# Thirty small loads added to a bandwidth-bound decode layer: fifteen ahead of the last head's K, fifteen behind the down weights

## The chip, the cores and the metric

The kernel runs on one core of one Trainium2 chip. The metric is the device time of one execution in microseconds (us); lower is better. A core has five engines, each with its own instruction stream: TensorE (PE in the profile, its weight loads as PEld), VectorE (DVE), ScalarE (ACT), GpSimd (POOL) and SyncE (SP). In this kernel SP computes nothing: it issues every transfer between the device memory (HBM) and the on-chip memory (SBUF, 128 partitions, here called rows of a tile). The transfers are carried by 16 DMA engines, which the profile reports together.

## The reference

One token is decoded through an attention block and a gated feed-forward block, with a residual around each. All is float32.

```
def _A_ref(x, k_cache, v_cache, wq, wo):
    B, Sq, D = x.shape
    H, Dh = 32, 192
    q = (x @ wq).reshape(B, Sq, H, Dh) -> (B, H, Sq, Dh)
    scores = einsum("bhqd,bhkd->bhqk", q, k_cache) * (Dh ** -0.5)
    p = softmax(scores, axis=-1)
    o = einsum("bhqk,bhkd->bhqd", p, v_cache)
    return o -> (B, Sq, H * Dh) @ wo

def _B_ref(x, W_gate, W_up, W_down):
    gate = einsum("bsd,df->bsf", x, W_gate)
    up = einsum("bsd,df->bsf", x, W_up)
    gate = gate * (gate > 0)
    return einsum("bsf,fd->bsd", gate * up, W_down)

h = x + _A_ref(layernorm(x), ...)
h2 = h + _B_ref(layernorm(h), ...)
```

(The transposes are written here as arrows.) The sizes are D = 640, 32 heads of 192, 8192 cached positions for each head, and a feed-forward width of 1536. The K and V caches are 6.3 MB a head each, over 400 MB together. Every byte of them is used once.

## The kernel before, in words

**Tiling.** The host packs all inputs into a few arrays of 128 rows (`row_p`, `row_1` to `row_5`, `row_t1`, `row_t2a`, `row_t2b`, `row_t3`, `row_up`, `row_gate`, `row_down`), so that one DMA takes one long contiguous piece from each row into each of the 128 partitions. In SBUF there are three slots of 65,280 bytes a partition, X, Y and Z (`slot_x`, `slot_y`, `slot_z`). K, V and the weights of a head live in pieces of these slots, and a piece is overwritten as soon as the engines have read it.

**The loop.** Head 0 is done ahead. A loop of ten turns does heads 1 to 30, three a turn, with five loads a turn of 7.6 to 8.2 MB each. Then comes a tail that is written out: the last head's K and the first part of the V of the head before it (`row_t1`, into X), more V and an output weight (`row_t2a`, into Z), the first half of the last head's V (`row_t2b`, into Z behind it), the second half (`row_t3`, into Y), the feed-forward's up weights (`row_up`, Y), its gate weights (`row_gate`, X), and its down weights in four pieces (`row_down`, X).

**Who waits for whom.** Each load has a semaphore that rises to 16 when its data have landed, and each reader waits for it (`land`, `tl`). In the other direction an engine that has read a piece raises a semaphore (`free`, `fin`), and SP waits for it ahead of the load that overwrites the piece. SP's program is a list in this order, and one waiting instruction holds all loads behind it. `sync_program` is that list, `load` issues one DMA, and `turn(i)` issues a turn's loads 3, 4 and 5 and then waits for the two semaphores (`free[2]`, `free[4]`) that release X and Z to the loads that follow.

**TensorE.** `pe_k` computes a half of a head's scores (12 matmuls), `pe_v` the product of the probabilities with V, 32 blocks of 384 columns a head, any stretch of them from `i0` to `i1`; it can raise a semaphore with one of its matmuls (`inc_at`). In the tail `pe_v(vz, 0, 16)` reads the first half of the last head's V from Z, and it is the last reader of Z. The output is 640 numbers in `o2`, copied by DVE and ACT (semaphore `fout`), and stored by SP in a transfer of two rows.

Of the kernel before, what the change touches and what calls it, by code (L numbers as in the profile page):

```python
# [88 lines left out]
def build(nc, arrays):  # L89
    dram = {k: nc.dram_tensor(k, v.shape, F32, kind="ExternalInput").ap() for k, v in arrays.items()}  # L90
    out = nc.dram_tensor("out", (1, 1, D), F32, kind="ExternalOutput").ap()
    sb = lambda name, shape: nc.alloc_sbuf_tensor(name, list(shape), F32).ap()

    slot_w = 16320
    X, Y, Z = (sb(n, [P, slot_w]) for n in ("slot_x", "slot_y", "slot_z"))
# [23 lines left out]
    gu = sb("gu", [P, FG])  # L119
    guT = sb("guT", [P, FJ, 32])  # L120
    o2 = sb("o2", [P, 2 * DG])

    ps = lambda name, w: nc.alloc_psum_tensor(name, [P, w], F32).ap()
    sc = ps("sc", 1024)
# [2 lines left out]
    sem = nc.alloc_semaphore  # L127
# [3 lines left out]
    free = [sem(f"free{i}") for i in range(6)]  # L131
    tl = {n: sem(f"tl_{n}") for n in ("t1", "t2a", "t2b", "t3", "up", "gate", "d0", "d1", "d2", "d3")}
    fin, fout, hsem = (sem(n) for n in ("fin", "fout", "hsem"))
    cst_pe, cst_ve, hdve, hrs, out_s = (sem(n) for n in ("cst_pe", "cst_ve", "hdve", "hrs", "out_s"))

    def wait(eng, s, n, sub=0, **kw):
        w = eng.wait_ge(s, n)  # L137
        if sub:
            w.then_inc(s, -sub)
        return w  # L140

    def op(ins, w=None, inc=None):
        if w is not None:
            ins._wait_ge(*w)
        if inc is not None:
            ins.then_inc(inc, 1)
        return ins
# [22 lines left out]
    vz = lambda i: cut(Z, W_T2A + i * PW, PW) if i < 16 else cut(Y, (i - 16) * PW, PW)  # L170
# [16 lines left out]
    def pe_v(blk, i0, i1, last=None, inc_at=None):  # L187
        for i in range(i0, i1):
            g = i % 4
            m = te.matmul(po[32 * g:32 * g + 2, 0:PW], p[:, 2 * i:2 * i + 2], blk(i), start=(i < 4), stop=(i >= 28))  # L190
            if inc_at is not None and i == inc_at[0]:
                op(m, inc=inc_at[1])
            if i == 31 and last is not None:
                op(m, inc=last)
# [60 lines left out]
    def tensor_program():  # L255
# [21 lines left out]
        wait(te, a2p, 1, 1)  # L277
        pe_l()
        wait(te, tl["t2b"], 16, 16)
        pe_v(vz, 0, 16)  # L280
        wait(te, d2p, 3, 3)
        for g in range(4):
            te.matmul(acc[Q(g), 0:DG], ones[Q(g), 0:32], xd[Q(g)].rearrange("p c j -> p (c j)"),
# [289 lines left out]
    sp = nc.sync  # L573

    def load(t, src, s):
        sp.dma_start(t, src).then_inc(s, 16)

    def sync_program():
        r1, r2, r3, r4, r5 = (dram[f"row_{i}"] for i in range(1, 6))

        def turn(i):
            wait(sp, free[5], 1, 1)
            wait(sp, land[5], 16, 16)
            load(Y[:, 0:W_3], r3[i], land[3])
            wait(sp, free[1], 2, 2)
            load(X[:, 0:W_4], r4[i], land[4])
            wait(sp, free[3], 2, 2)
            load(Y[:, 0:W_5], r5[i], land[5])
            wait(sp, free[2], 1, 1)
            wait(sp, free[4], 1, 1)  # L590

        with sp.Fori(0, NTURN - 1) as i:
            turn(i)
            load(X[:, 0:W_1], r1[i + 1], land[1])
            load(Z[:, 0:W_2], r2[i + 1], land[2])
        turn(NTURN - 1)
        load(X[:, 0:W_T1], dram["row_t1"], tl["t1"])
        load(Z[:, 0:W_T2A], dram["row_t2a"], tl["t2a"])
        load(Z[:, W_T2A:W_T2A + W_T2B], dram["row_t2b"], tl["t2b"])
        wait(sp, free[5], 1, 1)  # L600
        wait(sp, land[5], 16, 16)
        load(Y[:, 0:W_T3], dram["row_t3"], tl["t3"])
        load(Y[:, W_T3:W_T3 + W_UP], dram["row_up"], tl["up"])
        wait(sp, fin, 1, 1)
        load(X[:, 0:W_UP], dram["row_gate"], tl["gate"])
        for n, (a, b) in enumerate(DOWN):
            load(X[:, W_UP + a:W_UP + b], dram["row_down"][:, a:b], tl[f"d{n}"])
        wait(sp, fout, 2)
        load(out[0, 0].rearrange("(g n) -> g n", g=2), o2[31:33, :], out_s)
        wait(sp, fout, 2, 2)  # L610
        wait(sp, out_s, 16, 16)

    programs = ((ET.PE, tensor_program), (ET.DVE, vector_program), (ET.Activation, scalar_program),
                (ET.Pool, pool_program), (ET.SP, sync_program))
    load(Y[:, 0:W_P], dram["row_p"], land[5])
    load(X[:, 0:W_1], dram["row_1"][0], land[1])
# [16 lines left out]
```

## Time and profile before

| what | value |
|---|---|
| median of 3 runs | 1037.67 us (1037.61 to 1037.70) |
| the profiled execution's own time | 1037.78 us |
| its span, first to last instruction | 1036.5 us |
| read from HBM | 445.94 MB, 430 GB/s over the span |
| SP's DMA queue, share of 16 engines' span | 99.6% |
| PE busy | 548.8 us (53%) |
| DVE busy, ACT busy | 188.4 us (18%), 41.5 us (4%) |

How to read it: the span is what the trace covers, and the profiled execution took 1.28 us more than its span, spent ahead of the first and behind the last traced instruction. "SPq" is a row of SP's own instruction stream, "DMA_DIRECT2D" a DMA being issued, and its duration is the time in which SP issues it, not the time of the transfer. "To landing" counts from that issue until the last of the transfer's semaphore counts has come. A window's "DMA share" is the time of the packets that start in it, over 16 engines; a packet here is one row's piece, or the four bytes of a semaphore count. A short window in which many long packets start can show a share above 1.

### The profile page before, as it was taken

The numbers are of one execution on the slowest core, as the hardware profiler recorded it, in microseconds if no ns is written. First come the engines' busy times: TensorE is split into PE (matmuls) and PEld (weight loads), VectorE is DVE, ScalarE is ACT, GpSimd is POOL, SyncE is SP. The second block draws the span as 40 slices with busy tenths as digits, with TensorE's granted clock in tenths as the row PEclk, the third lists the DMA queues.
The fourth block names the chain that finished last, engine by engine and source line by source line (L and its number), as shares of the span: only waits on it lengthen the run. The fifth ranks groups of instructions, "written<-read, shape, count | busy, mean of one in ns | idle before, by whom it ended". The sixth has DMA issues, their size and how long they took to land. (4 is left out here: it accounts for less than half of the span.)

```text
span 1036.5 us, 10312 instructions
## 1 busy us (share of the span) xinstructions
PE 548.8 (53%) x4532; PEld 182.0 (18%) x4532; DVE 188.4 (18%) x479; ACT 41.5 (4%) x138; POOL 2.0 (0%) x13
## 2 busy tenths in 40 slices
PE   0745546455474463564644636646455465464667
PEld 0211112111121121121111202211111111121123
DVE  1301211111222022121111220211222012111211
ACT  1000000000000000000000000000000000000000
POOL 0000000000000000000000000000000000000000
PEclk9877867868776687687676876767767767678698
DMA  9999999999999999999999999999999999999998
GB/s 403 441 433 428 432 436 432 441 423 436 429 444 423 439 438 432 423 443 434 436 423 442 431 438 432 426 435 441 427 428 436 439 425 432 441 432 440 422 426 352
DMA packets 8796, 446.07 MB, mean 430 GB/s; under 512 B 978, under 2 KB 1108, under 8 KB 1236
## 3 DMA queue, kind: packets, MB, share of 16 engines
q1 hardware_dynamic: 8788, 445.95, 99.6%
q8 instruction: 7, 0.11, 0.0%
q14 instruction: 1, 0.01, 0.0%
HBM read 445.94 MB, written 0.00 MB: 430 GB/s over the span
## 5 line engine op out<-in xcount | busy, mean ns | idle before, releaser
L183 PE MATMUL sc<-slot_x,qs 128*32 128x512 f32 x1008 | 147.1, 727 | 88.1 <-PEq L137 88.1
L190 PE MATMUL po<-slot_y,p 128*2 128x384 f32 x1152 | 126.2, 594 | 83.7 <-DMA slot_y<-row 79.3
L190 PE MATMUL po<-slot_z,p 128*2 128x384 f32 x560 | 68.3, 638 | 103.9 <-PEq L137 103.9
L183 PE MATMUL sc<-slot_y,qs 128*32 128x512 f32 x288 | 56.2, 944 | 85.4 <-PEq L137 85.4
L190 PE MATMUL po<-slot_x,p 128*2 128x384 f32 x336 | 43.6, 652 | 82.0 <-PEq L137 82.0
L406 DVE STREAM_TRANSPOSE st<-sc 128x512 f32<-128x512 f32 x64 | 45.7, 713 | 168.7 <-PE sc L183 168.7
L183 PEld LDWEIGHTS sc<-slot_x,qs 128*32 128x32 f32 x1008 | 36.0, 131 | 169.1 <-issue 168.7
L190 PEld LDWEIGHTS po<-slot_y,p 128*2 128x2 f32 x1152 | 32.9, 98 | 177.2 <-DMA slot_y<-row 88.4
L394 DVE COPY oc<-od 128x2 f32<-128x2 f32 x32 | 5.1, 159 | 225.6 <-PE od L209 225.6
L412 DVE TENSOR_REDUCE m<-pt 128x1 f32<-128x128 f32 x32 | 9.3, 292 | 193.6 <-PE pt L202 193.6
L190 PEld LDWEIGHTS po<-slot_z,p 128*2 128x2 f32 x560 | 14.8, 99 | 148.0 <-issue 146.7
L518 ACT COPY qs<-q_ps 128x96 f32<-128x96 f32 x32 | 7.6, 238 | 772.6 <-PE q_ps L199 772.6
L388 DVE SCALAR_TENSOR_TENSOR prod<-slot_y,xn,prod 128x192 f32<-128x192 f32 x88 | 36.9, 419 | 3.1
L183 PEld LDWEIGHTS sc<-slot_y,qs 128*32 128x32 f32 x288 | 13.0, 157 | 114.7 <-issue 114.7
L401 DVE RECIPROCAL rl<-pl 128x1 f32<-128x1 f32 x32 | 5.4, 168 | 130.7 <-PE pl L214 128.0
L183 PE MATMUL sc<-slot_z,qs 128*32 128x512 f32 x240 | 27.6, 592 | 0.0
L190 PEld LDWEIGHTS po<-slot_x,p 128*2 128x2 f32 x336 | 9.0, 95 | 105.1 <-issue 105.1
L206 PE MATMUL od<-mrl,ob 128*128 128x1 f32 x132 | 20.0, 256 | 8.7 <-PEq L137 8.7
L206 PEld LDWEIGHTS od<-mrl,ob 128*128 128x128 f32 x132 | 17.6, 194 | 34.0 <-issue 34.0
L521 ACT COPY ob<-po 128x384 f32<-128x384 f32 x32 | 15.3, 478 | 177.0 <-PE po L190 177.0
L386 DVE TENSOR_SCALAR prod<-slot_y,xn 128x192 f32<-128x192 f32 x22 | 6.9, 315 | 67.2 <-DMA slot_y<-row 67.2
L197 PE MATMUL q_ps<-pat,prod 128*128 128x96 f32 x64 | 15.3, 322 | 7.1 <-PEq L137 7.1
(101 smaller groups left out, 262.6 us busy)
## 6 DMA issues: line engine op xcount, KB each, us to landing
slot_x<-row SPq DMA_DIRECT2D x10, 8160.0 KB, 26.8
slot_z<-row SPq DMA_DIRECT2D x10, 8160.0 KB, 45.7
slot_y<-row SPq DMA_DIRECT2D x10, 8160.0 KB, 45.3
slot_x<-row SPq DMA_DIRECT2D x10, 7680.0 KB, 35.6
slot_y<-row SPq DMA_DIRECT2D x10, 7584.0 KB, 26.9
slot_x<-row_t SPq DMA_DIRECT2D x1, 7680.0 KB, 26.3
slot_y<-row_p SPq DMA_DIRECT2D x1, 7136.0 KB, 19.8
slot_z<-row_t2a SPq DMA_DIRECT2D x1, 5088.0 KB, 38.3
```

Source lines behind the costliest of these rows:

```text
L183: m = te.matmul(sc[Q(g), half * 512:half * 512 + 512], qs[:, 32 * part:32 * part + 32], blk(half, part * 4 + g), start=(part == 0), stop=( ...
L190: m = te.matmul(po[32 * g:32 * g + 2, 0:PW], p[:, 2 * i:2 * i + 2], blk(i), start=(i < 4), stop=(i >= 28))
L197: te.matmul(q_ps[:, 0:96], prod[:, 0:P], pat[:, 0, :], start=True, stop=False)
L206: te.matmul(od[:, 0:1], ob[:, k * DH:k * DH + P], mrl[:, k:k + 1], start=(k == 0), stop=(k == 1))
L386: dv(ve.tensor_scalar(prod, w3[:, 0, :], xn[:, 0:1], None, op0=ALU.mult), w=first)
L388: dv(STT(prod, w3[:, j, :], xn[:, j:j + 1], prod, op0=ALU.mult, op1=ALU.add), w="self", inc=d2p if j == DJ - 1 else None)
L394: dv(ve.tensor_copy(oc, od[:, 0:2]), w=pd())
L401: dv(ve.reciprocal(vec["rl"], pl[:, 0:1]), w=pd())
L406: return dv(ve.transpose(st[:, s], sc[:, s]), w=w)
L412: dv(ve.reduce_max(vec["m1"], pt[:, 0:P], axis=AX.X, negate=True), w=pd(), inc=d2a)
L518: op(ac.copy(qs, q_ps[:, 0:96]), w=ap("p2a"), inc=a2p)
L521: op(ac.copy(ob, po[:, 0:PW]), w=ap("p2a"), inc=a2p)
```

## The change

Two groups of 15 DMAs are put in SP's list. The first stands between the last turn and the load of `row_t1`: load k, for k from 15 down to 1, takes 128 numbers (512 bytes) from each of the first k rows of `row_up` into a new tile `mark` that nothing reads. The second stands behind the down weights: the same with 192 numbers (768 bytes), into slot Z, which is dead by then. So that it is dead, the matmul of block 15 of `pe_v(vz, 0, 16)` raises a new semaphore `zfree`, and SP waits for it ahead of the second group. All thirty add to one semaphore, `msem`, which SP waits for at the end (30 times 16 is 480), behind the store and ahead of the wait for the store.

```
+    mark = sb("mark", [16, 2048])
+    msem, zfree = sem("msem"), sem("zfree")
...
-        pe_v(vz, 0, 16)
+        pe_v(vz, 0, 16, inc_at=(15, zfree))
...
         turn(NTURN - 1)
+        for k in range(15, 0, -1):
+            load(mark[0:k, 128 * k:128 * k + 128], dram["row_up"][0:k, 0:128], msem)
         load(X[:, 0:W_T1], dram["row_t1"], tl["t1"])
         load(Z[:, 0:W_T2A], dram["row_t2a"], tl["t2a"])
         load(Z[:, W_T2A:W_T2A + W_T2B], dram["row_t2b"], tl["t2b"])
...
         for n, (a, b) in enumerate(DOWN):
             load(X[:, W_UP + a:W_UP + b], dram["row_down"][:, a:b], tl[f"d{n}"])
+        wait(sp, zfree, 1, 1)
+        for k in range(15, 0, -1):
+            load(Z[0:k, 256 * k:256 * k + 192], dram["row_up"][0:k, 0:192], msem)
         wait(sp, fout, 2)
         load(out[0, 0].rearrange("(g n) -> g n", g=2), o2[31:33, :], out_s)
         wait(sp, fout, 2, 2)
+        wait(sp, msem, 480, 480)
         wait(sp, out_s, 16, 16)
```

How the rows stand on SP, at the first place, before: the last turn's loads 4 and 5 into X and Y, and then the tail's loads. A row gives the line, the tile, where it is loaded from, and rows times float32 numbers a row; the waits are those ahead of it.

```order
L576 DMA slot_x<-row_4 128x15360 [waits free1]
L576 DMA slot_y<-row_5 128x15168 [waits free3]
L576 DMA slot_x<-row_t1 128x15360 [waits free2,free4]
L576 DMA slot_z<-row_t2a 128x10176
L576 DMA slot_z<-row_t2b 128x6144
```

And with the change, the same place on SP:

```order
L578 DMA slot_x<-row_4 128x15360 [waits free1]
L578 DMA slot_y<-row_5 128x15168 [waits free3]
L578 DMA mark<-row_up 15x128 [waits free2,free4]
L578 DMA mark<-row_up 14x128
...
L578 DMA mark<-row_up 2x128
L578 DMA mark<-row_up 1x128
L578 DMA slot_x<-row_t1 128x15360
L578 DMA slot_z<-row_t2a 128x10176
L578 DMA slot_z<-row_t2b 128x6144
```

The wait for `free2` and `free4` now stands ahead of the first small load, and `row_t1` stands fifteen issues behind that wait.

The second place, SP behind the down weights, with the change (before, the store stood straight behind the last piece of the down weights):

```order
L578 DMA slot_x<-row_down 128x960
L578 DMA slot_x<-row_down 128x320
L578 DMA slot_z<-row_up 15x192 [waits zfree]
L578 DMA slot_z<-row_up 14x192
...
L578 DMA slot_z<-row_up 2x192
L578 DMA slot_z<-row_up 1x192
L578 DMA out<-o2 2x320 [waits fout]
```

A wait for `zfree` and fifteen issues now stand between the last load of weights and the store.

More of the change, by code (lines that the diff above doesn't have):

```diff
@@ L121, in build @@
     o2 = sb("o2", [P, 2 * DG])
+    mark = sb("mark", [16, 2048])
     ps = lambda name, w: nc.alloc_psum_tensor(name, [P, w], F32).ap()
@@ L133, in build @@
     fin, fout, hsem = (sem(n) for n in ("fin", "fout", "hsem"))
+    msem, zfree = sem("msem"), sem("zfree")
     cst_pe, cst_ve, hdve, hrs, out_s = (sem(n) for n in ("cst_pe", "cst_ve", "hdve", "hrs", "out_s"))
@@ L279, in tensor_program @@
         wait(te, tl["t2b"], 16, 16)
-        pe_v(vz, 0, 16)
+        pe_v(vz, 0, 16, inc_at=(15, zfree))
         wait(te, d2p, 3, 3)
@@ L596, in sync_program @@
         turn(NTURN - 1)
+        for k in range(15, 0, -1):
+            load(mark[0:k, 128 * k:128 * k + 128], dram["row_up"][0:k, 0:128], msem)
         load(X[:, 0:W_T1], dram["row_t1"], tl["t1"])
@@ L607, in sync_program @@
             load(X[:, W_UP + a:W_UP + b], dram["row_down"][:, a:b], tl[f"d{n}"])
+        wait(sp, zfree, 1, 1)
+        for k in range(15, 0, -1):
+            load(Z[0:k, 256 * k:256 * k + 192], dram["row_up"][0:k, 0:192], msem)
         wait(sp, fout, 2)
@@ L610, in sync_program @@
         wait(sp, fout, 2, 2)
+        wait(sp, msem, 480, 480)
         wait(sp, out_s, 16, 16)
```

## The prediction, made before the changed kernel had run

> **What bounds the kernel now.** The first view is the page's strip of 40 slices and its table of DMA queues:
>
> ```profile
> DMA  9999999999999999999999999999999999999998
> q1 hardware_dynamic: 8788, 445.95, 99.6%
> q8 instruction: 7, 0.11, 0.0%
> ```
>
> The 16 DMA engines are busy in every slice and SP's queue q1 fills 99.6% of their time, so the time is the bytes over the rate, plus whatever lets an engine run dry. The question is therefore whether the added loads leave one of the 16 engines without work, and whether that engine is one that ends late. The second view is the timeline of SP, which issues all transfers (start, duration, what is issued):
>
> ```profile
> 0.81 0.41 SPq L576 DMA_DIRECT2D slot_y<-row_p  x1
> 1.28 0.41 SPq L576 DMA_DIRECT2D slot_x<-row  x1
> 1.75 0.42 SPq L576 DMA_DIRECT2D slot_z<-row  x1
> ...
> 933.24 0.33 SPq L576 DMA_DIRECT2D slot_y<-row  x1
> 952.20 0.33 SPq L576 DMA_DIRECT2D slot_x<-row_t  x1
> 952.58 0.43 SPq L576 DMA_DIRECT2D slot_z<-row_t2a  x1
> 953.05 0.43 SPq L576 DMA_DIRECT2D slot_z<-row_t2b  x1
> ...
> 988.47 1.85 SPq L576 DMA_DIRECT2D slot_x<-row_down  x4
> 1035.35 0.33 SPq L576 DMA_DIRECT2D out<-o  x1
> ```
>
> An issue is not free. Issues in a row stand 0.47 us apart (0.81, 1.28, 1.75; 952.58, 953.05), the second after a wait 0.38 us behind the first (952.20, 952.58). At 952.20, where the change puts its first group, the queue holds one load: the one into Y issued at 933.24 (`row_5`). How long it lasts is seen in the windows of the DMA engines (stretch, its length, engines, clock, then DMA share and GB/s of the packets that start in it):
>
> ```profile
> 957.75:958.18 0.43, 0.00 (x0) 0.00 (x0) 0.00 (x0) 0.00 (x0) 0.00 (x0) 0.50 0.00 0
> 958.18:958.50 0.32, 0.00 (x0) 0.00 (x0) 0.00 (x0) 0.00 (x0) 0.00 (x0) 0.50 3.56 1536
> 958.50:958.80 0.30, 0.00 (x0) 0.00 (x0) 0.00 (x0) 0.00 (x0) 0.00 (x0) 0.50 0.95 410
> 958.80:959.30 0.50, 0.00 (x0) 0.00 (x0) 0.00 (x0) 0.00 (x0) 0.00 (x0) 0.50 0.85 369
> 959.30:959.70 0.40, 0.00 (x0) 0.00 (x0) 0.00 (x0) 0.00 (x0) 0.00 (x0) 0.50 0.00 0
> 959.70:960.00 0.30, 0.00 (x0) 0.00 (x0) 0.00 (x0) 0.00 (x0) 0.00 (x0) 0.50 1.43 614
> ```
>
> A row of `row_t1` is 61,440 bytes, so rate times length counts the engines that pass from `row_5` to `row_t1`: 8 at 958.2 to 958.5 (1536 GB/s in 0.32 us), 2 by 958.8, 3 by 959.3, none to 959.7, 3 by 960.0. The engines run up to 1.75 us apart, and the first runs out of `row_5` 6.0 us behind 952.20. Last, the end:
>
> ```profile
> 1031.40:1031.60 0.20, 0.20 (x15) 0.20 (x8) 0.00 (x0) 0.00 (x0) 0.00 (x0) 1.00 0.85 328
> 1031.60:1031.80 0.20, 0.20 (x8) 0.06 (x4) 0.00 (x0) 0.00 (x0) 0.00 (x0) 1.00 1.26 438
> 1031.80:1032.00 0.20, 0.20 (x8) 0.00 (x0) 0.00 (x0) 0.00 (x0) 0.00 (x0) 1.00 0.61 243
> 1032.00:1032.40 0.40, 0.40 (x8) 0.00 (x0) 0.00 (x0) 0.00 (x0) 0.00 (x0) 1.00 0.46 179
> 1032.40:1032.80 0.40, 0.17 (x4) 0.00 (x0) 0.00 (x0) 0.00 (x0) 0.00 (x0) 1.00 0.42 170
> 1032.80:1033.20 0.40, 0.20 (x8) 0.24 (x12) 0.00 (x0) 0.00 (x0) 0.00 (x0) 1.00 0.37 144
> 1033.20:1033.60 0.40, 0.40 (x20) 0.40 (x16) 0.00 (x0) 0.00 (x0) 0.00 (x0) 1.00 0.20 74
> 1033.60:1033.95 0.35, 0.35 (x19) 0.35 (x12) 0.00 (x0) 0.00 (x0) 0.00 (x0) 1.00 0.07 26
> ```
> ```profile
> q8 instruction: 1, 0.02, 0.4%
> ```
> ```profile
> 1034.41 0.48 PE L344 MATMUL q_ps<-slot_x,guT 128*32 128x80 f32 x16
> ```
>
> Share times length from 1031.60 on sums to 0.98 us, so a mean engine ends at 1032.58, and the last at 1033.95; TensorE's last matmuls start at 1034.41, straight behind it. The mean start of `row_t1` in the windows before (8 at 958.34, 2 at 958.65, 3 at 959.05, 3 at 959.85) is 958.80, so the tail is 73.78 us of work for a mean engine. In it fall instruction fetches on q8, here one in the 15 us from 1010: 0.4% of 16 engines is about 1.0 us of one engine. If the tail has four (of the page's seven, an estimate), they are a quarter of a us on the mean, and an engine without one needs 73.5 us. The last engine's 1033.95 less 73.5 is 960.4, later than any start. So it carried a fetch; less 1.0 gives 959.4, and I place it in the group at 959.05, with 1.4 us for its fetch and what this holds up. The bounds are the other groups, 958.35 and 959.85.
>
> **The change, part by part. First group.** Fifteen issues now stand ahead of `row_t1`. No 15-row issue is in the trace, but the two-row store is (1035.35): 0.33 us, like the 128-row issue after a wait at 952.20. So I take the spacing of 128-row issues, 0.47 us; the low bound is 0.37, the store's 0.33 and a little for decoding, an estimate. `row_t1` is then issued at 952.20 + 0.38 + 14 x 0.47 = 959.16 (low: 952.20 + 15 x 0.37 = 957.75). From an issue into an empty queue to its first packet:
>
> ```profile
> 1.30:1.84 0.54, 0.00 (x0) 0.00 (x0) 0.04 (x1) 0.54 (x1) 0.54 (x1) 1.00 0.00 0
> 1.84:2.10 0.26, 0.00 (x0) 0.00 (x0) 0.00 (x0) 0.25 (x1) 0.26 (x2) 1.00 7.99 2415
> 2.10:2.54 0.44, 0.00 (x0) 0.00 (x0) 0.00 (x0) 0.00 (x0) 0.37 (x5) 1.00 1.75 649
> ...
> 1036.00:1036.12 0.12, 0.00 (x0) 0.00 (x0) 0.00 (x0) 0.00 (x0) 0.00 (x0) 1.00 0.06 22
> ```
>
> The first load, issued at 0.81, starts on 11 engines from 1.84 (2415 GB/s in 0.26 us, in rows of 57,088 bytes) and on the other 5 by 2.54: 1.03 to 1.73 us. The store's two packets start by 1036.12: at least 0.65 us. So `row_t1` starts at R between 959.8 and 960.9; I take 960.4. Every engine has run out of `row_5` by then or just does, so all start level at R, and any that carries a fetch ends 960.4 - 959.05 = 1.35 us later than the last one does now. The term is **+1.35 us**, bounds +0.75 and +1.85, or with the other groups 0 and +2.5; at 0.37 us an issue R is 958.4 to 959.5, a shift of 0 to 0.45.
>
> The Trainium skill (DMA: Bandwidth & Descriptors, Latency and other measured facts) gives about 600 ns to the first byte of a load issued by SP. By it R would be 959.76 and the term about +0.7, 1038.4 in all. The trace has longer delays, above all 1.03 to 1.73 us for a load on all 16 engines, and these stand in the sum.
>
> The data of the small loads weigh little. Their price is bounded by the last two down weights:
>
> ```profile
> slot_y<-row SPq DMA_DIRECT2D x1, 7584.0 KB, 27.2
> slot_x<-row_t SPq DMA_DIRECT2D x1, 7680.0 KB, 26.3
> slot_y<-row_up SPq DMA_DIRECT2D x1, 3840.0 KB, 42.3
> slot_z<-row_t2a SPq DMA_DIRECT2D x1, 5088.0 KB, 38.3
> ...
> slot_x<-row_down SPq DMA_DIRECT2D x1, 480.0 KB, 44.6
> slot_x<-row_down SPq DMA_DIRECT2D x1, 160.0 KB, 44.5
> ```
>
> The four down issues start at 988.47, 988.94, 989.41 and 989.88, so the last two land at 1034.0 and 1034.4: 0.4 us for eight rows of 1280 bytes and a semaphore count on each engine, 50 ns a row. A 512-byte row costs 20 ns by bytes, at most 50. With one row an engine and load, an engine gets at most 15: 0.3 to 0.75 us, inside its gap ahead of R (959.85 + 0.75 is 960.6). Without that gap they would be added.
>
> Behind `row_t1` on SP wait `row_t2a` and `row_t2b`, which move with it but have 18 us of `row_t1` ahead of them. TensorE's wait for the last K moves from 978.5 (952.20 + 26.3) by 1.35 us, and with it the gate load at 988.1; but the up weights are on the queue until 1015.7 (973.43 + 42.3; that issue is not shown), so it stays covered by over 20 us.
>
> **Second group.**
>
> ```profile
> 998.34 2.76 PE L190 MATMUL po<-slot_z,p 128*2 128x384 f32 x32 [0.97 <-PEq L137]
> ```
>
> `zfree` comes with these matmuls at 1001.1; fifteen issues end at about 1008, 27 us ahead of the store's. Their rows queue behind the last down weights, at most 15 of 768 bytes an engine, 30 to 50 ns each: 0.45 to 0.75 us behind 1033.95. The store's packets come at 1036.1, 2.15 us behind it, so nothing is late; without that cover it is +0.75. The last wait ends under the store's own landing: 0. **Sum** +1.35 us: 1037.78 becomes 1039.1 in the profiled execution, and against the median of the runs, 0.11 lower, 1037.67 becomes 1039.0.
>
> **The rivals. The queue holds back (slower).** At 989.88 nine loads were in flight (`row_t2a` landed at 990.9, and eight behind it), with no longer issues. The change has 17 when `row_t1` is issued. If the queue takes 16, that issue waits until `row_5` has landed at 960.4 (933.24 + 27.2); R becomes 961.1 to 962.1, +2.0 to +3.1 us: 1039.7 to 1040.8. If it takes nine, seven small ones stand behind that as well, 3.3 us more: 1043 to 1044. For it speaks that no more than nine were ever seen; against it, that some seventy rows and counts waited on each engine then, more than this group would put there.
>
> **Each small load costs its engine a round trip (slower).** From the store's issue to the span's end are 1.15 us; fifteen in series are 17 us on one engine. They stand behind `row_5` in its queue, so all of them would delay `row_t1` there: about 1054. The two down weights that landed 0.4 us apart speak against it. A rule of the Trainium skill (DMA: Bandwidth & Descriptors, Rules for kernel authors) would have it so in kind: small transfers are to be coalesced, and under 64 KB one pays mostly overhead. The largest here has 7.5 KB; the trace shows the overhead in SP's issues, not on the queue.
>
> **The small issues are quicker (no change).** At 0.37 us or below, `row_t1` arrives as the engines run out, and 0 to +0.45 us is left: 1037.6 to 1038.1. For it speaks the 0.33 us of the store, against it the 0.43 us of every issue that follows another.
>
> **The loads level the engines (faster).** If small rows held up only engines that end early, and the fetches fell on others, the last end could move forward to the mean engine's: 1.4 us at most, 1036.3.
>
> **How the numbers follow.** Forecast 0.63, queue holds back 0.13, round trips 0.03, quicker issues 0.18, levelled 0.03. The forecast's own range is 1038.2 to 1039.9. The whole range reaches down to the quicker issues and up to a queue of 16: 1037.5 to 1040.7. A measurement of this kernel can tell 0.2%, 2.1 us, from no change: faster 0.01, slower 0.25 (queue, round trips, and 0.09 of the forecast's upper end), same 0.74.
>
> **What would show it.** In the changed profile SP's small issues stand 0.47 us apart and `row_t1` is issued near 959.2; windows from 958.5 to 960 show DMA shares far below 1 with only small packets, and all 16 engines start long rows within a us. `row_t1` and all later loads land 1 to 2 us later. Spacings below 0.4, or no gap, make the third rival right; one long issue among the fifteen, the first.

## The result, and the profile after

The changed kernel takes 1039.66 us (median of 18 executions, 1038.71 to 1040.37) against 1037.66 us for the kernel before in the same comparison: a ratio of 1.0019, 95% interval 1.0013 to 1.0026, or 2.0 us more. Its executions scatter over 1.7 us, those of the kernel before over 0.8 us. The profiled execution took 1039.70 us, with a span of 1038.5 us against 1036.5.

SP's timeline of the changed kernel, the rows that answer to those shown of before:

```profile
932.55 0.33 SPq L578 DMA_DIRECT2D slot_y<-row  x1
953.21 5.31 SPq L578 DMA_DIRECT2D mark<-row_up  x15
958.57 0.36 SPq L578 DMA_DIRECT2D slot_x<-row_t  x1
...
989.93 1.90 SPq L578 DMA_DIRECT2D slot_x<-row_down  x4
1003.08 16.95 SPq L578 DMA_DIRECT2D slot_z<-row_up  x15
1037.10 0.25 SPq L578 DMA_DIRECT2D out<-o  x1
```

Fifteen issues took 5.31 us, 0.36 us each with the gaps between them, not 0.47. SP began them at 953.21, 1.0 us later than it issued `row_t1` before, so `row_t1` went out at 958.57 after all. The later start comes from TensorE, whose granted clock (third number from the right) differed between the two executions in the 8 us ahead of it; the first row is of the kernel before, the second of the changed one:

```profile
945.00:953.00 8.00, 7.01 (x66) 2.49 (x58) 1.94 (x6) 0.87 (x3) 0.00 (x0) 0.96 0.95 410
```
```profile
945.00:953.00 8.00, 8.00 (x66) 2.66 (x58) 1.17 (x4) 0.87 (x3) 0.00 (x0) 0.83 0.95 410
```

Of this stretch, the 24 matmuls on slot X that TensorE begins at 945.1 took 3.00 us before and 4.02 us here, which is the whole delay.

At the second place SP needed 16.95 us for fifteen issues, far more than the 7 us forecast. By form (shortest, median and longest, in ns) the two groups read:

```profile
L578 SPq DMA_DIRECT2D mark<-row_up x15: 253/297/407, 953.2 to 958.3; - x15
```
```profile
L578 SPq DMA_DIRECT2D slot_z<-row_up x15: 312/526/2249, 1003.1 to 1017.8; - x15
```

An issue of over 2 us is SP being held. Now the DMA engines where `row_5` ends, in windows of the changed kernel:

```profile
957.75:958.18 0.43, 0.00 (x0) 0.00 (x0) 0.00 (x0) 0.00 (x0) 0.00 (x0) 0.67 0.00 0
958.18:958.80 0.62, 0.00 (x0) 0.00 (x0) 0.00 (x0) 0.00 (x0) 0.00 (x0) 0.50 0.27 61
958.80:959.50 0.70, 0.00 (x0) 0.00 (x0) 0.00 (x0) 0.00 (x0) 0.00 (x0) 0.50 0.11 25
959.50:960.00 0.50, 0.00 (x0) 0.00 (x0) 0.00 (x0) 0.00 (x0) 0.00 (x0) 0.50 4.35 1361
960.00:960.60 0.60, 0.12 (x4) 0.11 (x8) 0.14 (x1) 0.00 (x0) 0.00 (x0) 0.50 1.35 515
960.60:962.20 1.60, 1.60 (x12) 0.30 (x8) 1.46 (x5) 0.00 (x0) 0.00 (x0) 0.50 0.00 0
962.20:963.40 1.20, 1.20 (x12) 0.30 (x8) 1.20 (x3) 0.00 (x0) 0.00 (x0) 0.50 1.89 819
```

From 958.2 to 959.5 only small packets start (25 to 61 GB/s); then 11 engines begin `row_t1` by 960.0 (1361 GB/s in 0.5 us, 61,440 bytes each) and 5 by 960.6. The gap and the level restart are there. But a row at the usual pace lasts 2.27 us, so second rows were due from 961.8 on, and none starts before 962.2. The first long rows are slow as well: in the trace's packets they last 2.27 to 3.53 us, 2.95 in the mean. At the end:

```profile
slot_x<-row_down SPq DMA_DIRECT2D x1, 480.0 KB, 44.9
slot_x<-row_down SPq DMA_DIRECT2D x1, 160.0 KB, 44.8
```
```profile
1036.17 0.49 PE L346 MATMUL q_ps<-slot_x,guT 128*32 128x80 f32 x16
...
1037.10 0.25 SPq L578 DMA_DIRECT2D out<-o  x1
```

The last piece of the down weights was the fourth issue of the 1.90 us from 989.93 and landed at about 1036.2, where it landed at 1034.4 before; the last matmuls (1034.41 before) and the store (1035.35) moved by 1.75 us with it.

Which engine ends last can be followed. A packet in the trace names no engine, but on one engine each packet starts 3 to 4 ns ahead of the recorded end of the one before it, so the rows of each engine can be linked from `row_t1` to the end of the gate weights. Before, 13 engines need 68.74 to 68.77 us for this stretch. Three carry an instruction fetch in it and need 70.29 to 70.31 us, and these three come out last. The latest of them starts `row_t1` at 958.93 and comes out at 1029.24. In the changed kernel, too, the latest engine carries a fetch. It starts `row_t1` at 960.23, 1.30 us later; its first row lasts 2.70 us, 0.44 us longer than usual; it comes out at 1030.80, 1.56 us later, the rest of its way having taken 0.17 us less.

### The profile page after: what moved, and what is told of

Same layout as the page of the kernel before. It is cut to its first block, busy times and chain, and to the rows that moved or that the text cites. A ratio compares the mean times of both kernels' runs of the same rounds, so it can differ in the third digit from the quotient of the medians.

```text
span 1038.5 us, 10344 instructions
## 1 busy us (share of the span) xinstructions
PE 543.7 (52%) x4532; PEld 181.4 (17%) x4532; DVE 188.5 (18%) x479; ACT 41.4 (4%) x138; POOL 2.0 (0%) x13
## 5 line engine op out<-in xcount | busy, mean ns | idle before, releaser
L185 PE MATMUL sc<-slot_x,qs 128*32 128x512 f32 x1008 | 149.7, 738 | 96.0 <-PEq L139 96.0
L192 PE MATMUL po<-slot_y,p 128*2 128x384 f32 x1152 | 117.6, 560 | 82.0 <-DMA slot_y<-row 77.8
L192 PE MATMUL po<-slot_z,p 128*2 128x384 f32 x560 | 71.3, 662 | 101.2 <-PEq L139 101.2
L185 PE MATMUL sc<-slot_y,qs 128*32 128x512 f32 x288 | 53.4, 904 | 83.8 <-PEq L139 83.8
```

Of the source, the lines that this page charges most:

```text
L185: m = te.matmul(sc[Q(g), half * 512:half * 512 + 512], qs[:, 32 * part:32 * part + 32], blk(half, part * 4 + g), start=(part == 0), stop=( ...
```

## The experiments

The theory at the start was the forecast's: the loss is the late issue of `row_t1`. Its rivals were that the small loads themselves hold up the queue, and that the second group costs something. The diffs are against the kernel before, except where another is named; each kernel was timed beside it.

**The first group alone.**

```
+        for k in range(15, 0, -1):
+            load(mark[0:k, 128 * k:128 * k + 128], dram["row_up"][0:k, 0:128], msem)
         load(X[:, 0:W_T1], dram["row_t1"], tl["t1"])
```

> The first group alone. Late-issue theory (the whole cost is that row_t1 is issued some 5 us later, so that the DMA engines run dry between row_5 and row_t1): nearly all of the loss stays, 1039.3 to 1039.7 against 1037.7 before, and the executions scatter over 1 us or more, since the issue now hangs on the moment at which TensorE releases X. Queue-data theory (the small rows themselves hold up the DMA engines): the same here. Second-group theory (fifteen loads behind the down weights hold SP and meet the last rows): a good part goes, 1038.7 or less.

Measured: 1039.29 us (1038.68 to 1040.30) against 1037.49; ratio 1.0017, 1.0008 to 1.0027. Most of the loss is in the first group. The profiled execution is one of its quicker ones, 1038.81 us, and shows something that the theory doesn't have:

```profile
951.99 5.31 SPq L578 DMA_DIRECT2D mark<-row_up  x15
957.34 0.36 SPq L578 DMA_DIRECT2D slot_x<-row_t  x1
```
```profile
958.18:958.80 0.62, 0.00 (x0) 0.00 (x0) 0.00 (x0) 0.00 (x0) 0.00 (x0) 0.50 3.67 1062
958.80:959.50 0.70, 0.00 (x0) 0.00 (x0) 0.00 (x0) 0.00 (x0) 0.00 (x0) 0.50 0.82 277
```

Here TensorE released X at 952.0, `row_t1` went out at 957.34, and ten engines begin it by 958.80: there is little gap. Yet the execution took 1.3 us more than the kernel before.

**The second group alone.**

```
+        wait(sp, zfree, 1, 1)
+        for k in range(15, 0, -1):
+            load(Z[0:k, 256 * k:256 * k + 192], dram["row_up"][0:k, 0:192], msem)
         wait(sp, fout, 2)
```

> The second group alone, the first left out. Late-issue theory: 1037.6 to 1037.9, no more than 0.2 us of loss, though SP shows issues of 2 us among the fifteen, which nothing waits for. Second-group theory: 1038.2 or more.

Measured: 1038.01 us (1037.58 to 1038.17) against 1037.49; ratio 1.0004, 0.9995 to 1.0013. It is between the two expectations, and the interval holds no change. Half of the 0.5 us lies outside the traced span: the time less the span is 1.45 to 1.55 us in all eleven executions, against 1.20 to 1.30 in the 33 of the kernel before. The other half is in the span, 1036.5 us in the median against 1036.2. In the changed kernel the time less the span is 1.19 to 1.37 us, 1.24 in the mean, so the first half is no part of its loss. What it is the traces don't show.

**The first group one load later, behind row_t1.**

```
         load(X[:, 0:W_T1], dram["row_t1"], tl["t1"])
+        for k in range(15, 0, -1):
+            load(mark[0:k, 128 * k:128 * k + 128], dram["row_up"][0:k, 0:128], msem)
```

> The first group alone, moved one load back: row_t1 is issued first, then the fifteen. The rows stand in the same queue, behind row_t1 in place of ahead of it, and the fifteen issues take SP's time while row_t1 is under way. Late-issue theory: 1037.5 to 1038.1 (at most the 0.45 us that fifteen rows at 30 ns take on the engine that has all fifteen, if that engine ends late). Queue-data theory: as much loss as with the first group in its place, 1039.3 or more.

Measured: 1038.47 us (ten executions, 1038.22 to 1038.96; an eleventh, at 2437.82, stands apart without an explanation and is left out) against 1037.49; ratio 1.0009, 1.0000 to 1.0019. Both theories miss: 1.0 us of loss stays with `row_t1` issued on time.

**The first group ahead of SP's wait.**

```
             load(Y[:, 0:W_5], r5[i], land[5])
+            if ahead:
+                for k in range(15, 0, -1):
+                    load(mark[0:k, 128 * k:128 * k + 128], dram["row_up"][0:k, 0:128], msem)
             wait(sp, free[2], 1, 1)
             wait(sp, free[4], 1, 1)
```

> The first group alone, moved ahead of SP's wait for the release of X and Z: issued at about 933 us, straight behind row_5, while SP would only wait. The rows stand in the queue between row_5 and row_t1, just as in the change. Late-issue theory: 1037.5 to 1038.1, and a narrow scatter. Queue-data theory: 1039.3 or more.

Measured: 1038.70 us (1038.27 to 1040.03) against 1037.49; ratio 1.0012, 1.0003 to 1.0021. Again 1.2 us, with SP's issues at 934.4 to 939.8 and nothing waiting for them. So some 1.0 to 1.2 us belong to the loads on the queue where the engines don't run dry. The 1.8 us of the first group in its place is some 0.6 us more, though the two intervals overlap. That the late issue simply adds these 0.6 us is argued, and the next run speaks against it.

**No small load, a late issue.**

```
+        wait(sp, land[5], 16)
         load(X[:, 0:W_T1], dram["row_t1"], tl["t1"])
```

> No small load at all; SP waits for row_5's landing ahead of row_t1, so that row_t1 is issued near 960.5 us in place of 952.2. Late-issue theory: the first long rows of row_t1 start at 961.4 to 962.4 on all engines, and the time is 3.2 to 4.2 us over before, 1040.9 to 1041.9, with a narrow scatter, since the issue hangs on a transfer and not on TensorE. Queue-data theory: nothing is added to the queue, 1037.7.

Measured: 1041.16 us (1040.88 to 1041.44) against 1037.49; ratio 1.0036, 1.0022 to 1.0051. The time is in the late-issue theory's range. SP issued `row_t1` at 960.23:

```profile
960.23 0.33 SPq L576 DMA_DIRECT2D slot_x<-row_t  x1
```

and its first packets start at 961.19 to 961.94, 1.0 to 1.7 us later. But the gap is not all of the cost. These are windows of the same execution:

```profile
961.19:961.95 0.76, 0.76 (x8) 0.15 (x4) 0.70 (x2) 0.00 (x0) 0.00 (x0) 0.50 3.85 1293
961.95:963.46 1.51, 1.51 (x16) 0.39 (x12) 1.50 (x3) 0.00 (x0) 0.00 (x0) 0.63 0.00 0
963.46:964.05 0.59, 0.59 (x12) 0.19 (x8) 0.17 (x1) 0.00 (x0) 0.00 (x0) 1.00 0.00 0
964.05:964.75 0.70, 0.70 (x16) 0.19 (x8) 0.00 (x0) 0.00 (x0) 0.00 (x0) 1.00 3.25 1404
```

All 16 engines begin `row_t1` in the first window (1293 GB/s in 0.76 us). At 2.27 us a row, second rows were due from 963.46 on, and none starts before 964.05. The first rows last 2.27 to 3.47 us, 2.93 in the mean, with no small load in the kernel. So engines that have run dry and start again together have a slow first row, as in the changed kernel (2.95). Linked as above, the engine that comes out last starts 2.47 us later than the last one before (961.40 against 958.93), its first row is 0.82 us longer, and it comes out 3.14 us later. The start of the kernel before has the same, again without small loads:

```profile
1.84:2.54 0.70, 0.00 (x0) 0.00 (x0) 0.00 (x0) 0.25 (x1) 0.63 (x5) 1.00 4.07 1305
2.54:3.95 1.41, 0.00 (x0) 0.00 (x0) 0.37 (x1) 0.00 (x0) 0.17 (x4) 1.00 0.00 0
3.95:4.56 0.61, 0.00 (x0) 0.00 (x0) 0.00 (x0) 0.00 (x0) 0.00 (x0) 1.00 0.00 0
4.56:5.60 1.04, 0.00 (x0) 0.00 (x0) 0.00 (x0) 0.00 (x0) 0.00 (x0) 1.00 2.03 878
```

Its second rows last 2.11 us; its first rows, of the same 57,088 bytes, last 2.29 to 3.57.

**Seven of the fifteen.** In the first group alone, `range(15, 0, -1)` becomes `range(7, 0, -1)`.

> The first group cut to its last seven loads (7 rows down to 1). Seven issues take about 2.3 us, so row_t1 is issued near 955, 3 us ahead of the first engine's end of row_5. Late-issue theory: no engine runs dry, 1037.6 to 1038.0. Queue-data theory: 28 of 120 rows and 7 of 15 loads are left, a loss of 0.4 us (by rows) to 0.9 us (by loads): 1038.1 to 1038.6.

Measured: 1037.51 us (1037.38 to 1037.88) against 1037.49; ratio 1.0000, 0.9991 to 1.0010. No cost in time, neither for the issues nor for seven loads on the queue. But the loads are not free to the engines. Linked packets show first rows of 2.27 to 2.31 us on engines with up to four small loads, 2.36 with five, 2.48 with six and 2.90 with seven. The three engines that come out last, each with a fetch, had none, none and two.

**Thirty narrow loads.** In the first group alone:

```
-        for k in range(15, 0, -1):
-            load(mark[0:k, 128 * k:128 * k + 128], dram["row_up"][0:k, 0:128], msem)
+        for k in range(30, 0, -1):
+            n = (k + 1) // 2
+            load(mark[0:n, 64 * k:64 * k + 64], dram["row_up"][0:n, 0:64], msem)
```

> The first group as thirty loads of half the width: each count of rows from 15 down to 1 twice, 256 bytes a row. The bytes are the same, the issues and the semaphore counts are doubled. Late-issue theory: fifteen more issues at some 0.35 us move row_t1 back by 5.3 us, and since the engines are dry already, all of that goes to the end: 1044.5 to 1045.5. Queue-data theory by bytes: 1039.7; by loads: 1041.7.

Measured: 1044.40 us (1043.22 to 1044.95, four executions) against 1037.49; ratio 1.0063, 1.0046 to 1.0080. Just under what the late-issue theory gave: once the engines are dry, fifteen more issues cost 5.1 us over the first group alone, where SP takes 5.4 us for them at 0.36 us each. A price for fifteen more loads on the queue, which would come on top, doesn't show.

Two things were now open: why fifteen loads cost where seven do not, and whether the price is that of short rows or of loads. Four runs took these apart, all with SP's issues hidden or harmless.

**Fifteen loads on all engines.** As the first group ahead of SP's wait, with `mark[0:16, ...]` and `dram["row_up"][0:16, ...]` in place of `0:k`.

> The fifteen loads ahead of SP's wait, each of 16 rows, so that every one of the 16 engines has fifteen small rows and fifteen semaphore counts. Run-length theory, by rows or by loads: all engines are held up by 0.45 us of packets and 1.6 us in the next long row, and the engine that ends last with them: 1039.2 to 1039.7. If only some engines can be held up (those that run early): 1038.6, as with 15 rows down to 1.

**The same rows in two loads.**

```
+                for k in range(2):
+                    load(mark[:, 128 * k:128 * k + 128], dram["row_up"][:, 128 * k:128 * k + 128], msem)
```

> In place of the fifteen, two loads of 128 rows of 512 bytes, ahead of SP's wait: sixteen small rows on every engine, but only two semaphore counts. Run-length theory by rows (the price is that of a short row): every engine is held up as the one with fifteen was, 1038.9 to 1039.7. Run-length theory by loads (the price is that of a load's own semaphore count or start): the sixteen rows take 0.45 us and no more, 1037.7 to 1038.1.

Measured: fifteen loads 1039.89 us (1039.61 to 1040.10), ratio 1.0023, 1.0014 to 1.0033; two loads 1037.83 us (1037.55 to 1038.12), ratio 1.0003, 0.9994 to 1.0012; before 1037.50 for both. Every engine moves 15 short rows in the one and 16 in the other, of the same 512 bytes. Two loads cost 0.33 us, fifteen 2.39 us. So the price is not that of a short row: 13 loads more cost 2.06 us, some 0.16 us each. Two other things differ in this pair, and no run varied them alone: the fifteen loads all read the first 512 bytes of the same 16 rows and write into 16 partitions, while the two read and write all 128 rows. The price does not show in the small packets but in the long row behind them. The windows of the kernel with fifteen loads, and then of that with two:

```profile
960.00:960.60 0.60, 0.00 (x0) 0.00 (x0) 0.01 (x1) 0.00 (x0) 0.00 (x0) 0.50 1.75 451
960.60:962.20 1.60, 1.59 (x12) 0.40 (x16) 1.49 (x4) 0.00 (x0) 0.00 (x0) 0.50 0.00 0
962.20:963.40 1.20, 1.20 (x12) 0.29 (x8) 1.17 (x3) 0.00 (x0) 0.00 (x0) 0.50 1.18 512
```
```profile
960.00:960.60 0.60, 0.04 (x4) 0.05 (x8) 0.06 (x1) 0.00 (x0) 0.00 (x0) 0.50 0.78 327
960.60:962.20 1.60, 1.60 (x12) 0.36 (x16) 1.50 (x4) 0.00 (x0) 0.00 (x0) 0.50 1.15 499
962.20:963.40 1.20, 1.20 (x12) 0.30 (x8) 1.17 (x4) 0.00 (x0) 0.00 (x0) 0.50 1.42 614
```

With two loads, 13 second rows start between 960.6 and 962.2 (499 GB/s in 1.6 us). With fifteen none does, though the first rows began at 958.5: they last 3.46 to 4.40 us in the trace's packets, where all 16 last 2.27 us behind two loads. With the first group alone the slowest first row, behind fifteen loads, lasts 3.9 us, though some of its engines run dry first, which is slow by itself.

**The fifteen spread.** Loads of 15 to 11 rows ahead of SP's wait, 10 to 6 behind `row_t1`, 5 to 1 behind `row_t2a`:

```
+        def small(a, b):
+            for k in range(a, b - 1, -1):
+                load(mark[0:k, 128 * k:128 * k + 128], dram["row_up"][0:k, 0:128], msem)
...
         load(X[:, 0:W_T1], dram["row_t1"], tl["t1"])
+        small(10, 6)
         load(Z[:, 0:W_T2A], dram["row_t2a"], tl["t2a"])
+        small(5, 1)
```

> The first group alone, its fifteen loads spread: 15 to 11 rows behind row_5 and ahead of SP's wait, 10 to 6 rows behind row_t1, 5 to 1 rows behind row_t2a, so that no engine has more than five in a run. Run-length theory (an engine hides the first five or six small loads of a run, and each further one lengthens its next long row by some 0.16 us): 1037.5 to 1037.9. Fixed-price theory (each small load costs its engine the same wherever it stands): 1038.6 to 1038.8, as with all fifteen ahead of the wait.

Measured: 1038.15 us (1037.76 to 1038.35) against 1037.50; ratio 1.0006, 0.9997 to 1.0015. Between the two: 0.65 us in place of the 1.2 us of one run. Five in a run are not free (long rows of 2.3 to 2.6 us behind them), but cheaper each than fifteen.

**Seven loads behind the down weights.** The second group alone with `range(7, 0, -1)`.

> The second group alone, cut to its last seven loads (7 rows down to 1), so that SP's issues are not held up. If the half us of the whole second group comes from its length (the full queue, or what it leaves to do at the end): 1037.4 to 1037.6. If it comes from the wait for zfree or the last wait: 1037.9 to 1038.1, as with the whole group.

Measured: 1037.50 us (1037.27 to 1037.65) against 1037.50; ratio 1.0000, 0.9991 to 1.0009. If the second group's half us is real, it belongs to its length, not to its two waits. What in its length, the traces don't show.

## Why the prediction was right or wrong

The time lies in the range, the sign of the term is right, and 2.0 us against a forecast of 1.35 is under the 0.2% that the forecast took as the bound of a measurable change. The mechanism is right: a late issue lets the engines run dry, and the run without small loads shows that this alone costs time. The size came out partly by luck, as one step was too long, one delay was not foreseen, and one term was put at nothing.

- **The gap and the level restart** were right: a profiled gap from 958.2 to 959.5, and all 16 engines on `row_t1` within 1.1 us. R was forecast as 960.4, bounds 959.8 and 960.9; the windows show 959.5 to 960.6. On the engine that comes out last the shift is 1.30 us, against 1.35.
- **The last engine and its fetch** were right: it starts at 958.93, where the forecast placed it at 959.05, and a fetch costs its engine 1.55 us (70.3 against 68.75 us), where the forecast had 1.4.
- **The spacing of issues** was mis-sized: 0.47 us forecast, 0.36 measured. That alone would have brought `row_t1` out at 957.6, near the rival of quicker issues. In the profiled execution TensorE's release came 1.0 us later, which gave most of it back; that is luck. That the first issue hangs on TensorE's clock was not in the forecast; it is in the two clock rows above, and it fits the wider scatter, though no run isolated it.
- **The delay from issue to packets** was right: 1.0 to 1.7 us without small loads, as at the start of the kernel.
- **The pace behind R** is the term that was put at nothing. The forecast let every engine go on from R as before, but the first rows after a restart are slow: 2.95 us in the mean in place of 2.27, and 0.44 us more on the engine that comes out last. It needs no small load (2.93 where SP waits for `row_5`), and the trace before had it at 1.84 to 4.56.
- **"The data of the small loads weigh little"** failed where the engines don't run dry. The forecast allowed 0.3 to 0.75 us on an engine without a gap; the fifteen cost 1.0 to 1.2 us there, and 2.4 us with fifteen on all engines. The packets do take no more than 30 ns a load, but a run of loads lengthens the next long row, by up to 1.7 us with one to fifteen loads and 2.1 with fifteen on all engines. In the changed kernel itself, where there is a gap, this price does not stand out: its first rows are as slow as those without small loads. The down weights, from which the price was taken, had eight rows to a load and could not show a price by load.
- **The rival of a round trip for each load** was nearer in kind than the forecast allowed and wrong in size: 0.16 us a load, less for the first few of a run, not 1.15 us. That each load makes a round trip is not shown. The rule named with it, in the Trainium skill (DMA: Bandwidth & Descriptors, Rules for kernel authors), to coalesce small transfers, is borne out by the pair of two and fifteen loads: 0.33 against 2.39 us for nearly the same bytes. The forecast set it aside too quickly.
- **The rival of a queue that holds back** came true at the other group. Seven loads of weights were still in flight there; the eighth small issue took 0.53 us and the seven after it 1.1 to 2.2 us each. SP was free again 17 us ahead of the store, as the forecast's cover of 27 us allowed. At the first group, with 16 loads in flight, nothing was held, so the bound is not on the number of loads; the rows and counts queued on an engine (some 70 where it was held, some 40 at the first group, worked out from the loads in flight) fit, but no run varied them alone.
- **"Nothing is late" behind the second group** is not refuted: the group alone has 0.3 us more in its span, with an interval that holds no change.

How the 2.0 us divide is not shown. Where SP waits for `row_5`, `row_t1` is issued 1.66 us later than in the changed kernel (960.23 against 958.57), and the loss is larger by 1.2 us between the profiled executions and by 1.7 between the medians. If each us of later issue costs a us, the late issue and its slow restart explain 1.4 to 2.0 us here without any small load; this is an estimate from these two kernels. The rest, 0 to 0.5 us, is left for the fifteen loads in their gap and for the second group. The 1.0 to 1.2 us that the loads cost without a gap are therefore not shown to be a term of it.

## What to carry to other kernels

On a kernel whose DMA queue never rests, a small load has two prices that its bytes don't show: the issuing engine's time, which counts in full once the queue runs dry behind it, and a price by load on each DMA engine that it uses, which appears in the next long transfer and counts if that engine ends late. A queue that runs dry costs more than the gap, since the first long rows behind it are slow too. Put the same rows into few loads, or few loads at a time, and issue them where the issuing engine would only wait. A price that is taken from packets of large loads does not hold for small ones; time the small ones alone first.

## What the runs showed of the hardware that was not expected

- Engines that have run dry and start again together have slow first rows, with no small load: 2.27 to 3.47 us, 2.93 in the mean, where a row at the usual pace lasts 2.27; and 2.29 to 3.57 at the start of the kernel, where it lasts 2.11.
- A run of small loads slows the long row behind it, with no gap: 2.27 us at its usual pace, 3.46 to 4.40 us behind fifteen loads on each engine, 2.27 us behind two loads with as many rows. Whether the load's semaphore count, its start, or the repeated source and the 16 partitions is the cause was not separated.
- SP's time for an issue falls with the rows: behind the first, 0.37 to 0.41 us from issue to issue at 14 to 10 rows, 0.29 to 0.32 us at one to three.
- SP can be held while it issues: up to 2.2 us an issue in the second group (3.4 with that group alone), and not at all for as many loads of as many rows in the first. The depth of the queue fits as the cause and was not varied alone.
